# Second pass of a split feed-forward layer: 512-token chunks, and seven block products of two ff tiles in place of eight

## The chip, the cores and the metric

The kernel runs on one core of a Trainium2 chip. Its five engines run side by side, each in the order of its own queue: TensorE (PE, matmuls into the PSUM banks; its weight loads are listed apart as PEld), VectorE (DVE), ScalarE (ACT), GpSimd (POOL, which works on SBUF alone here) and SyncE (SP), from which all transfers are issued. The metric is the device time of one execution in microseconds (us), as the median of three runs.

## The reference

Attention over 8 batches, 8 heads, 576 positions and 64 dimensions, with a causal window of 128, gives x, 4608 tokens by 512. Then follows a feed-forward layer with 2048 hidden columns:

```python
x = np.ascontiguousarray(attn_out.transpose(0, 2, 1, 3)).reshape(B * S, H * D)
h = x @ w_in                                  # 4608 x 2048
sp = np.maximum(h, 0.0) + np.log1p(np.exp(-np.abs(h)))
g = h * erf(sp)
return (g @ w_out).astype(np.float32)         # 4608 x 512
```

## The kernel before

The weights come as double-precision words and are rounded on the chip. Every matmul of the feed-forward layer is made of three passes, since an operand is split in a high part and the rest: high by high, high by rest, rest by high. So `whi`/`wli` are the two parts of a tile of w_in, `who`/`wlo` of w_out, `xh`/`xl` of x, and `gh`/`gl` of g.

Hidden columns are worked in 16 tiles of 128 ("ff tiles"), in two passes over the tokens, since the weights of all 16 don't fit beside the attention. The **first pass** takes tiles 0 to 5 and is woven into the attention; its partial results go to DRAM (`pd`). When the attention's buffers are closed, the weights of tiles 6 to 15 are prepared in their place, and the **second pass** takes these ten and adds the stored part. The changed piece is the second pass.

A chunk is 384 tokens (`CH`), so there are 12 chunks. For each chunk and ff tile there is one unit: twelve matmuls of 384 columns into one PSUM bank (`h`, line 782: four blocks of 128 rows of x, three passes each), a copy of the bank to `hs` by ACT or DVE (lines 766, 768), softplus and erf on ACT with a table load ahead of each (lines 811, 813; four units share a pair of table loads), a product on DVE (line 824), the rounding to `gh` (766, 768) and the rest `gl` (829), and nine matmuls of 512 columns (`o`, line 844: three tiles of 128 tokens, three passes each) that are summed over the ff tiles in three banks. At the end of a chunk each bank is added to the stored part (line 864) and leaves.

The order of all this is not written out. Every operation is entered with the engines that may do it, an assumed duration, the buffers that it reads and writes, and a due time; a planner (`Plan.run`) then lists the operations engine by engine, the earliest due first among those whose inputs and buffers are free. `at` is the due time. `hs`, `s`, `gh` and `gl` live in one pool of 17 buffers of 768 columns (tag `m`, `MB`), where `keep` says how many must stay free when one is taken. x is read into one buffer (`xr`) and split into `xh` and `xl`, three buffers each. `Weights.prepare` does the work for one tile of weights: one pass on ACT, four on DVE, one sum on POOL, then high part and rest (lines 670 to 692).

In PSUM the second pass uses two banks for h and three for o. The three banks of the attention stand empty by then.

Of the kernel before, what the change touches and what calls it, by code (L numbers as in the profile page):

```python
# [39 lines left out]
MB, KH, KS = 17, 4, 2  # L40
PB, XB, OB, TB, TBB = 8, 3, 3, 2, 2
# [268 lines left out]
def pool_tt(n):  # L310
    return 0.15 + n * 0.0025
# [334 lines left out]
class Weights:  # L646
# [9 lines left out]
    def prepare(self, which, f, at, after=()):  # L656
# [3 lines left out]
        q = Buf(self.stage, [P, DM], I32, "wq", 1, f"wq{nm}")  # L660
# [27 lines left out]
        op({"Act": act(DM), "DVE": dve(DM, True)}, lambda e: (  # L688
            nc.scalar.copy if e == "Act" else nc.vector.tensor_copy)(hi.all, flt(t)),
            r=[t, *after], w=[hi], at=at)  # L690
        op({"Pool": pool_tt(DM), **({"DVE": dve(DM)} if WLO else {})}, lambda e: (
            nc.gpsimd if e == "Pool" else nc.vector).tensor_tensor(lo.all, flt(t), hi.all, SUB),  # L692
            r=[t, hi, *after], w=[lo], at=at)
        self.t[which, f] = (hi, lo)


class Moe:
# [4 lines left out]
    def __init__(self, tc, plan, ctx, x_dram, part_dram, out):  # L702
# [11 lines left out]
        self.rounds = []  # L714
        for n, size, tail in zip((NF1, NF - NF1), UPR, ((), TAIL)):
            n = n * nch - sum(tail)
            self.rounds += [size] * (n // size) + [n % size] * (n % size > 0) + [*tail]

    def one_pass(self, weights, first, time):

        fs = weights.ffs
        for c in range(self.nch):
            at = time(self.U)
            x = self.load_x(c, first, at)
            po = [Buf(self.ps_o, [P, DM], F32, f"o{t}", 1, f"o{t}_{self.U}") for t in range(NTT)]
            for f in fs:
                u = self.unit(c, f, weights, x, po, f == fs[0], f == fs[-1], first, time(self.U))
                self.round.append(u)
                self.U += 1
                if len(self.round) == self.rounds[0]:  # L730
                    self.rounds.pop(0)
                    self.flush()

    def direct(self, c):

# [232 lines left out]
```

## Time and profile before

| | us |
|---|---|
| median of 3 runs | 1116.16 |
| lowest, highest | 1114.83, 1118.36 |
| the profiled execution: its time | 1118.25 |
| the profiled execution: its span in the trace | 1116.3 |
| last product of the attention starts (line 596, output `px`) | 521.8 |
| PE busy in the 112 us from 784 on | 112.00 |
| DVE, ACT busy in the same stretch | 40.43, 58.48 |

The span is the time from the first to the last event of the trace, and the execution's own time is a little longer. A matmul's duration in a row holds its way through the array, so rows of successive matmuls overlap: what a matmul costs in a dense stream is the distance from its start to the next one's start. "Busy" of PE is thus no proof of a dense stream, and the distances are. The rows that carry the argument stand in the prediction.

### The profile page before, as it was taken

How to read it: one execution, taken by the hardware profiler on the slowest of the kernel's cores; microseconds unless marked ns; L12 is line 12 of the kernel's file. 1: busy time of each engine (PE TensorE's matmuls, PEld its weight loads, DVE VectorE, ACT ScalarE, POOL GpSimd, SP SyncE). 2: the span in 40 equal slices, each digit the busy share in tenths (PEclk: the TensorE clock that was granted, in tenths of full speed). 3: DMA queues.
4: the chain of work that ended last, by engine and by line, in shares of the span. 5: the costliest groups of instructions: out<-in, count | busy, mean ns of one | idle time of the engine just before them, and what ended most of it. 6: DMA issues, size and time to landing. Idle time of an engine off the chain costs nothing.

```text
span 1116.3 us, 17069 instructions
## 1 busy us (share of the span) xinstructions
PE 1073.7 (96%) x6000; PEld 976.5 (87%) x6000; DVE 684.9 (61%) x1602; ACT 721.9 (65%) x1436; POOL 385.7 (35%) x464
## 2 busy tenths in 40 slices
PE   9776979999999999999999999999999999999998
PEld 8666968988899999999899998899999999999996
DVE  5878898887888888775867675333433433433332
ACT  6567667878788787776677675355455455455462
POOL 5776887646666566653333231000000000000000
PEclk9797999999999999999999999999999999999999
DMA  6444555444545455422343422202202202202102
GB/s 184 139 132 122 140 152 153 146 132 115 163 118 135 121 143 149 118 89 78 114 132 114 141 69 74 86 13 73 85 19 67 85 19 67 85 13 73 57 19 67
DMA packets 89732, 111.59 MB, mean 100 GB/s; under 512 B 45744, under 2 KB 59696, under 8 KB 89648
## 3 DMA queue, kind: packets, MB, share of 16 engines
q1 hardware_dynamic: 89648, 110.52, 33.5%
q8 instruction: 47, 0.77, 0.3%
q14 instruction: 37, 0.30, 0.1%
HBM read 82.18 MB, written 28.31 MB: 99 GB/s over the span
## 4 chain that ended last, share of the span: by engine, by line
PE 82%; DVE 9%; POOL 3%; DMA 2%; issue 2%; ACT 2%; POOLq 0%; SPq 0%; DVEq 0%; ACTq 0%
PE o L844 32%; PE h L782 31%; PE px L596 7%; PE s L511 5%; PE t L578 5%; POOL p L560 2%; DMA xr<-xd 2%; DVE p L522 1%; PE warm_ps L383 1%; DVE xl L759 1%; POOL wto L686 1%; DVE hs L824 1%; DVE gl L829 1%; PE s L497 1%; ACT p L532 1%
## 5 line engine op out<-in xcount | busy, mean ns | idle before, releaser
L782 PE MATMUL h<-xh,whi 128*128 128x384 f32 x768 | 262.5, 342 | 0.0
L782 PE MATMUL h<-xl,whi 128*128 128x384 f32 x768 | 259.2, 338 | 1.6 <-DVE xl L759 1.6
L782 PE MATMUL h<-xh,wli 128*128 128x384 f32 x768 | 259.7, 338 | 0.0
L560 POOL TENSOR_SCALAR p<-p,st 128x256 f32<-128x256 f32 (+2 forms) x320 | 194.0, 623 | 128.1 <-DVE st L550 108.1
L844 PE MATMUL o<-who,gh 128*128 128x512 f32 x576 | 228.8, 397 | 0.6 <-DVE ot L768 0.6
L844 PE MATMUL o<-who,gl 128*128 128x512 f32 x576 | 227.6, 395 | 1.2 <-DVE gl L829 1.2
L844 PE MATMUL o<-wlo,gh 128*128 128x512 f32 x576 | 227.3, 395 | 1.2 <-POOL wlo L692 0.7
L766 ACT COPY hs<-h 128x384 f32<-128x384 f32 x137 | 65.3, 477 | 215.1 <-PE h L782 214.6
L532 ACT ACTIVATE p<-p,st 128x256 f32<-128x256 f32 (+2 forms) x320 | 149.0, 468 | 24.5 <-DVE st L522 23.6
L782 PEld LDWEIGHTS h<-xl,whi 128*128 128x128 f32 x768 | 145.2, 189 | 8.7 <-DVE xl L759 2.1
L782 PEld LDWEIGHTS h<-xh,whi 128*128 128x128 f32 x768 | 145.3, 189 | 6.9 <-ACT hs L766 0.2
L782 PEld LDWEIGHTS h<-xh,wli 128*128 128x128 f32 x768 | 144.8, 189 | 0.2 <-POOL wli L692 0.2
L844 PEld LDWEIGHTS o<-who,gl 128*128 128x128 f32 x576 | 108.1, 188 | 25.4 <-DVE gl L829 2.1
L522 DVE CUSTOM_DVE_ANT_0 p<-s,bias_sb 128x256 f32<-128x256 f32 (+2 forms) x320 | 109.4, 378 | 33.4 <-PE s L511 21.6
L768 DVE COPY hs<-h 128x384 f32<-128x384 f32 x55 | 30.4, 554 | 160.8 <-PE h L782 160.8
L844 PEld LDWEIGHTS o<-wlo,gh 128*128 128x128 f32 x576 | 108.5, 188 | 17.9 <-POOL wlo L692 2.2
L844 PEld LDWEIGHTS o<-who,gh 128*128 128x128 f32 x576 | 108.6, 188 | 16.6 <-DVE ot L768 1.5
L824 DVE TENSOR_TENSOR hs<-s,hs 128x768 f32<-128x768 f32 x96 | 95.2, 1016 | 23.4 <-ACT s L813 23.4
L829 DVE TENSOR_TENSOR gl<-hs,gh 128x768 fp32r<-128x768 f32 x96 | 94.6, 989 | 15.5 <-ACT gh L766 14.7
L578 PE MATMUL t<-ident,p 128*128 128x128 f32 x544 | 85.7, 284 | 17.6 <-POOL p L560 11.8
L578 PEld LDWEIGHTS t<-ident,p 128*128 128x128 f32 x544 | 65.6, 147 | 30.4 <-POOL p L560 14.6
L466 POOL TENSOR_TENSOR a_None<-qr_None,a_None 64x576 fp32r<-64x576 f32 x48 | 76.4, 1592 | 25.7 <-DVE a_None L474 20.7
(80 smaller groups left out, 1653.1 us busy)
## 6 DMA issues: line engine op xcount, KB each, us to landing
xr<-xd SPq DMA_DIRECT2D x22, 768.0 KB, 4.3
kr_None<-k_t SPq DMA_DIRECT2D x48, 288.0 KB, 4.2
pd<-ot SPq DMA_DIRECT2D x36, 256.0 KB, 3.7
ot<-pd SPq DMA_DIRECT2D x36, 256.0 KB, 3.0
wri<-w_in SPq DMA_DIRECT2D x16, 512.0 KB, 3.8
wro<-w_out SPq DMA_DIRECT2D x16, 512.0 KB, 3.7
out_dram<-ot SPq DMA_DIRECT2D x32, 256.0 KB, 2.1
qr_None<-q_t SPq DMA_DIRECT2D x24, 288.0 KB, 3.1
```

The costliest lines, as they stand in the source:

```text
L466: op({"Pool": pool_tt(nq)}, lambda e, j=j, own=own, other=other: nc.gpsimd.tensor_tensor(a[j][other, :nq], q[own, :nq], a[j][own, :nq], SU ...
L511: nc.tensor.matmul(ps[:m, j, :n], lhsT=a[j][:, q0 : q0 + m], rhs=rhs[:, k0 : k0 + n], start=(o == 0), stop=(o == 1),)
L522: nc.vector.tensor_tensor_reduce(out=pt[:m, c0:c1, j, :], in0=blocks(src[j][0][:m, src[j][1], :n]), in1=blocks(self.bias[:m, c0 * 64 : c1 ...
L532: nc.scalar.activation(dst, dst, AF.Exp, bias=low[:m, j : j + 1], scale=-1.0, accum_out=total[:m, j : j + 1],)
L560: nc.gpsimd.tensor_scalar(dst, dst, totals[t][:m, j : j + 1], 1.0, op0=ALU.mult, op1=ALU.mult)
L578: nc.tensor.matmul(ps[:, col : col + P], lhsT=p[t][:, kb].rearrange("p j d -> p (j d)"), rhs=self.ident[:, :], is_transpose=True, start=no ...
L596: self.nc.tensor.matmul(dst[:, q0 - base : q1 - base], lhsT=v[:, blk], rhs=sb[sbi][:, off : off + q1 - q0], start=(blk == order[0][0]), st ...
L766: self.nc.scalar.copy(out, src)
L782: nc.tensor.matmul(ps[:, :CH], lhsT=ww[:, cs], rhs=xx[:, k], start=(k2 + k + n == 0), stop=(k2 + k + n == 4),)
L824: V if e == "DVE" else G).tensor_tensor(hs[:, :n], s[:, :n], hs[:, :n], ALU.mult),
L829: V if e == "DVE" else G).tensor_tensor(gl[:, :n], hs[:, :n], gh[:, :n], SUB),
L844: nc.tensor.matmul(po.all, lhsT=g[:, j, cs], rhs=w.all, start=(u["start"] and n == 0), stop=(u["end"] and n == 2),)
```

## The change

The second pass takes 512 tokens at a time (nine chunks), and two ff tiles together (five pairs for each chunk, 45 pairs in all). For a pair, h is a product of a 2 by 2 block matrix (two ff tiles by two halves of x's 512 rows) and another (the two halves of x's rows by two halves of the tokens). Each of the eight block products was six matmuls; now there are seven block products, of sums and differences of blocks (Strassen's scheme in Winograd's form). Their results are put together with adds.

- **Weights.** `pair` makes, from two rounded tiles, three of the four blocks as they are and four sums (S1 to S4), each with a high part and a rest. They stand where all weights of the second pass stood. The second pass's w_out tiles now go into the buffers of the first pass's weights, which are free when the first pass has used them for the last time.
- **x.** `second_x` loads 512 tokens (from two of the 384-token pieces), makes four differences T1 to T4 and splits seven blocks (`xb` 0 to 6: B11, T1, B21, T2, B22, T3, T4). Four of them lie in a pool of six, three in the pool `m`, as do the differences themselves.
- **h.** A product is six matmuls of 256 columns into half a PSUM bank (`b`); two products share a bank. Four banks take turns: the two of before and two of the attention's. Two products are copied, five are added on DVE straight from PSUM, and two adds have both inputs in SBUF (DVE or POOL).
- **After h.** Softplus, erf, product and split are done on 1024 columns for each pair, with two table loads each. The o products are the same three passes of 512 columns, on four token tiles (the fourth bank is the attention's third).
- **Buffers.** `m` has 12 buffers of 1024 columns in place of 17 of 768, for the first pass too. The due times of the second pass are set anew (`TN`, `XL2`, `XS2`).

```diff
-FIT = 8
-UPR = (4, 4)
-TAIL = (2, 2)
+UPR = 4
+CH2, HALF = 512, 256
-MB, KH, KS = 17, 4, 2
-PB, XB, OB, TB, TBB = 8, 3, 3, 2, 2
+MB, KH, KS, KX = 12, 4, 2, 4
+PB, XB, OB, TB, TBB = 8, 6, 3, 2, 2
...
-        q = Buf(self.stage, [P, DM], I32, "wq", 1, f"wq{nm}")
+        q = Buf(self.stage, [P, DM], I32, "wq", 2, f"wq{nm}")
...
+    def pair(self, f, values, at, after):
...
+        (ta, flt), (tb, _) = (self.rounded(0, f + i, at) for i in range(2))
+        sums = Buf(values, [P, 4, HALF], F32, "m", MB, f"ws{f}", keep=KX)
+        pool, tag = self.place(0, f)
+        hi = Buf(pool, [P, 7, HALF], F32R, "h" + tag, 1, f"wh{f}")
+        lo = Buf(pool, [P, 7, HALF], F32R, "l" + tag, 1, f"wl{f}")
...
+        for k, x, y, sub, r in (
+            (0, lambda: flt(tb)[:, one], lambda: flt(tb)[:, two], False, [tb]),
+            (1, lambda: S(0), lambda: flt(ta)[:, one], True, [ta, parts[0]]),
+            (2, lambda: flt(ta)[:, one], lambda: flt(tb)[:, one], True, [ta, tb]),
+            (3, lambda: flt(ta)[:, two], lambda: S(1), True, [ta, parts[1]]),
+        ):
...
+    def second_x(self, d, at):
...
+        raw = Buf(self.xp, [P, NK, CH2], F32, "xr", 1, f"xr{d}_2")
...
+            pool, tag, bufs, keep = (self.xp, "xs", XB, None) if k < 4 else (self.hp, "m", MB, KX)
+            both = Buf(pool, [P, 2, 2, HALF], F32R, tag, bufs, f"xb{d}_{k}", keep=keep)
...
+        split("B11", 0)
+        sub("T1", 0, "B12", "B11")
+        split("T1", 1)
+        split("B21", 2)
+        sub("T2", 1, "B22", "T1")
+        split("T2", 3)
+        split("B22", 4)
+        sub("T3", 2, "B22", "B12")
+        split("T3", 5)
+        sub("T4", 3, "B21", "T2")
+        split("T4", 6)
...
+    def second_pair(self, Q, d, f, weights, x, po, spare, start, end, at):
...
+        hs = Buf(self.hp, [P, 2, CH2], F32, "m", MB, f"hs_q{Q}", keep=KH)
...
+            i, half = divmod(self.P, 2)
+            self.P += 1
+            if not half:
+                pool, tag, n = ((self.ps_h, "h", 2), (self.ps_h, "h", 2), (spare, "t", 1), (spare, "x", 1))[i % 4]
+                self.bank = Buf(pool, [P, 512], F32, tag, n, f"b{i}")
+            to = Part(self.bank, slice(None), slice(half * HALF, (half + 1) * HALF))
...
+            def mm(e):
+                for kk in range(2):
+                    cs = slice(kk * P, (kk + 1) * P)
+                    for n, (ww, xx) in enumerate(((hi, xh), (hi, xl), (lo, xh))):
+                        nc.tensor.matmul(
+                            to.all, lhsT=ww[:, k, cs], rhs=xx[:, kk],
+                            start=(kk + n == 0), stop=(kk + n == 3),
+                        )
...
+        copy(h11, product("A11", "B11", x["T4"]))
+        add(h12, product("S2", "T2"), h11)
+        add(h21, product("S3", "T3"), h12)
+        copy(h22, product("S1", "T1"))
+        add(h11, product("A12", "B21"), h11)
+        add(h12, h12, h22)
+        add(h22, h21, h22)
+        add(h21, product("A22", "T4"), h21)
+        add(h12, product("S4", "B22"), h12)
+        g = self.values([(f"_q{Q}", 2, CH2, [*H.values()], hs, at + MC)], False)[0]
+        for j in range(2):
+            last = end and j == 1
+            for t in range(NT2):
+                self.products(weights.t[1, f + j], j, t, g, po[t], start and j == 0, last, at + MP)
...
     place = lambda k, f: (
-        (pool2, f"{k}_{f}") if f < NF1 + FIT else (w1p, f"{k}_{f - NF1 - FIT}")
+        (pool2, f"2_{f}") if k == 0 else (w1p, f"{(f - NF1) // NF1}_{(f - NF1) % NF1}")
     )
```

How the change moves instructions is seen at three places. A row gives the line, the operation, output and inputs with the number of each buffer, the size, and a count of equal rows. First PE in the middle of the second pass of before: the o group of one unit ends, and the h group of the next begins.

```order
L844 MATMUL o_142_9655<-who_7413,gh_9606 128x512
L844 MATMUL o_142_9655<-wlo_7420,gh_9606 128x512
L844 MATMUL o_142_9655<-who_7413,gl_9612 128x512
L782 MATMUL h_9726<-xh_0_9424,whi_6551 128x384
L782 MATMUL h_9726<-xl_0_9433,whi_6551 128x384
L782 MATMUL h_9726<-xh_0_9424,wli_6572 128x384
```

PE now, where the second pass goes from its third chunk to its fourth: the end of the last product of the old chunk (`xb_4_8301`), then the first three products of the new chunk's first pair (T2, T1 and B21).

```order
L994 MATMUL b_8774<-xb_4_8301,wh_7012 128x256 x2
L994 MATMUL b_8774<-xb_4_8301,wl_7024 128x256
L994 MATMUL b_8783<-xb_3_8722,wh_6563 128x256 x2
L994 MATMUL b_8783<-xb_3_8722,wl_6566 128x256
L994 MATMUL b_8783<-xb_3_8722,wh_6563 128x256 x2
L994 MATMUL b_8783<-xb_3_8722,wl_6566 128x256
L994 MATMUL b_8793<-xb_1_8398,wh_6563 128x256 x2
L994 MATMUL b_8793<-xb_1_8398,wl_6566 128x256
L994 MATMUL b_8793<-xb_1_8398,wh_6563 128x256 x2
L994 MATMUL b_8793<-xb_1_8398,wl_6566 128x256
L994 MATMUL b_8793<-xb_2_8715,wh_6563 128x256 x2
```

A matmul is narrower, and its weights change as often as before. Two products stand behind each other in one bank (`b_8793`). Behind these rows follow, in this order: the rest of that product, two groups of three o matmuls, the product with `xb_5`, two groups, the one with the new `xb_4`, ten groups, and the products with `xb_0` and `xb_6`, which end the first pair of the new chunk.

DVE of before, where the second half of a chunk's x is split (`xl_1_9383`) between products and rests of g.

```order
L824 TENSOR_TENSOR hs_9284<-s_9314,hs_9284 128x768
L759 TENSOR_TENSOR xl_1_9383<-xr_0_9086,xh_1_9375 128x768
L829 TENSOR_TENSOR gl_9393<-hs_9227,gh_9378 128x768
L829 TENSOR_TENSOR gl_9405<-hs_9284,gh_9385 128x768
L768 CAST xh_0_9424<-xr_0_9391 128x768
L759 TENSOR_TENSOR xl_0_9433<-xr_0_9391,xh_0_9424 128x768
```

DVE now, at the same change from the third chunk to the fourth as on PE. `hs_q_8696` and `hs_q_8751` are the last two pairs of the old chunk.

```order
L1010 TENSOR_TENSOR hs_q_8751<-b_8774,hs_q_8751 128x256
L808 CAST xb_5_8811<-xt_1_8790 128x512
L940 TENSOR_TENSOR xb_5_8811<-xt_1_8790,xb_5_8811 128x512
L872 TENSOR_TENSOR hs_q_8696<-s_q_8764,hs_q_8696 128x1024
L1010 TENSOR_TENSOR hs_q_8751<-b_8755,hs_q_8751 128x256
L808 CAST gh_q_8837<-hs_q_8696 128x1024
L879 TENSOR_TENSOR gl_q_8849<-hs_q_8696,gh_q_8837 128x1024
L808 CAST xb_0_8857<-xr_2_8808 128x512
L940 TENSOR_TENSOR xb_0_8857<-xr_2_8808,xb_0_8857 128x512
L872 TENSOR_TENSOR hs_q_8751<-s_q_8839,hs_q_8751 128x1024
L808 CAST xb_6_8879<-xt_1_8790 128x512
L940 TENSOR_TENSOR xb_6_8879<-xt_1_8790,xb_6_8879 128x512
```

The adds from PSUM are new on DVE, and the x of a chunk is made in seven pieces, the last of them (`xb_6`) behind two products that wait for ACT.

More of the change, by code (lines that the diff above doesn't have):

```diff
@@ L687, in prepare @@
            r=[q, t], w=[t], at=at)
[L688 to L693, printed above, removed]
-        self.t[which, f] = (hi, lo)
+        return t, flt
@@ new lines, in split @@
+    def split(self, n, src, hi, lo, r, at, after=()):
+        nc, op = self.nc, self.plan.op
+        op({"Act": act(n), "DVE": dve(n, True)}, lambda e: (
+            nc.scalar.copy if e == "Act" else nc.vector.tensor_copy)(hi.all, src()),
+            r=[*r, *after], w=[hi], at=at)
+        op({"Pool": pool_tt(n), **({"DVE": dve(n)} if WLO else {})}, lambda e: (
+            nc.gpsimd if e == "Pool" else nc.vector).tensor_tensor(lo.all, src(), hi.all, SUB),
+            r=[*r, hi, *after], w=[lo], at=at)
@@ L713, in __init__, with first_pass @@
         self.round = []
[L714 to L719, printed above, removed]
+    def first_pass(self, weights, time):
         fs = weights.ffs
@@ L802, in flush @@
             us = units[k : k + 2]
-            n = len(us)
-            hs, U, at = us[0]["hs"], us[0]["U"], us[0]["at"] + MC
-            s = Buf(self.hp, [P, 2, CH], F32, "m", MB, f"s{U}", keep=KS)
-            pairs.append((us, n, n * CH, hs, s, at))
-        first = units[0]["first"]
+            pairs.append((us[0]["U"], len(us), CH, [us[0]["hs"]], us[0]["hs"], us[0]["at"] + MC))
+        for (U, n, ch, _, hs, at), g in zip(pairs, self.values(pairs, True)):
+            for j, u in enumerate(units[U - units[0]["U"] :][:n]):
+                for t in range(NTT):
+                    self.products(u["w"], j, t, g, u["po"][t], u["start"], u["end"], u["at"] + MP)
+                    if u["end"]:
+                        self.store_part(u["U"], self.part[u["c"]][t], u["po"][t], u["at"] + MP)
@@ new lines, in values, with products @@
+        return out
+    def products(self, w, j, t, g, po, start, end, at):
+        wh, wl = w
+        gh, gl = g
+        def mm(e):
+            cs = slice(t * P, (t + 1) * P)
+            for n, (g, w) in enumerate(((gh, wh), (gh, wl), (gl, wh))):
+                self.nc.tensor.matmul(
+                    po.all, lhsT=g[:, j, cs], rhs=w.all, start=(start and n == 0), stop=(end and n == 2),
+                )
+        self.plan.op({"PE": 3 * f32r_us(DM) + 0.015}, mm, r=[gh, gl, wh, wl], w=[po], at=at)
@@ new lines, in second_pass @@
+    def second_pass(self, weights, spare, time):
+        fs = weights.ffs
+        Q = self.P = 0
+        for d in range(len(self.x_dram) * CH // CH2):
+            x = self.second_x(d, time(Q))
+            po = [
+                Buf(self.ps_o, [P, DM], F32, f"o{t}", 1, f"o{t}_d{d}") if t < NTT
+                else Buf(spare, [P, DM], F32, "s", 1, f"o{t}_d{d}") for t in range(NT2)
+            ]
+            for f in fs[::2]:
+                self.second_pair(Q, d, f, weights, x, po, spare, f == fs[0], f == fs[-2], time(Q))
+                Q += 1
@@ new lines, in store_part, with store, rows @@
+    def store_part(self, U, part, po, at):
+        nc, op = self.nc, self.plan.op
+        ot = Buf(self.op_, [P, DM], F32, "o", OB, f"ot_{part.name}_{U}")
+        op({"DVE": dve(DM), "Act": act(DM, src=0.13)},
+           lambda e: self.copy(e, ot.all, po.all), r=[po], w=[ot], at=at)
+        op(emit=lambda e: nc.sync.dma_start(part.ap, ot.all), r=[ot], w=[part], at=at, **dma(P * DM * 4))
+    def store(self, nm, c, t, po, at):
+        nc, op = self.nc, self.plan.op
+        ot = Buf(self.op_, [P, DM], F32, "o", OB, f"ot{nm}")
+        part = self.part[c][t]
+        op(emit=lambda e: nc.sync.dma_start(ot.all, part.ap), r=[part], w=[ot], at=at - 10,
+           **dma(P * DM * 4))
+        op({"DVE": dve(DM)}, lambda e: nc.vector.tensor_tensor(
+            ot.all, po.all, ot.all, ALU.add), r=[po, ot], w=[ot], at=at)
+        def rows(e):
+            for o, r0, n in rows_of(c, t):
+                nc.sync.dma_start(self.out[r0 : r0 + n, :], ot[o : o + n])
+        op(emit=rows, r=[ot], at=at, **dma(P * DM * 4, len(rows_of(c, t))))
```

218 lines of the change are left out of this document (135 added, 83 removed).

## The prediction, made before the changed kernel was run

> **What bounds the kernel now.** I read the page first: busy shares, and the chain of work that ended last.
>
> ```profile
> PE 1073.7 (96%) x6000; PEld 976.5 (87%) x6000; DVE 684.9 (61%) x1602; ACT 721.9 (65%) x1436; POOL 385.7 (35%) x464
> ...
> PE 82%; DVE 9%; POOL 3%; DMA 2%; issue 2%; ACT 2%; POOLq 0%; SPq 0%; DVEq 0%; ACTq 0%
> PE o L844 32%; PE h L782 31%; PE px L596 7%; PE s L511 5%; PE t L578 5%; POOL p L560 2%; DMA xr<-xd 2%; DVE p L522 1%; PE warm_ps L383 1%; DVE xl L759 1%; POOL wto L686 1%; DVE hs L824 1%; DVE gl L829 1%; PE s L497 1%; ACT p L532 1%
> ```
>
> The feed-forward matmuls carry 63% of the chain. The change is in the second pass, so I ask that part, and the hand-over to it, for the busy time of each stretch.
>
> ```profile
> core 0: us, PE busy (x) PEld busy (x) DVE busy (x) ACT busy (x) POOL busy (x), PEclk, DMA share, GB/s
> 504.00:560.00 56.00, 54.55 (x290) 48.51 (x290) 38.80 (x66) 34.50 (x61) 19.23 (x19) 1.00 0.28 92
> 560.00:616.00 56.00, 56.00 (x284) 50.89 (x283) 41.17 (x57) 42.79 (x55) 18.84 (x14) 1.00 0.38 122
> 616.00:672.00 56.00, 56.00 (x294) 52.07 (x293) 37.12 (x60) 39.00 (x54) 18.61 (x14) 1.00 0.35 113
> ...
> 896.00:1008.00 112.00, 112.00 (x562) 101.39 (x562) 41.32 (x51) 58.03 (x74) 0.00 (x0) 1.00 0.16 52
> ```
>
> PE never rests from 560 on, at a full granted clock (1.00), while DVE is busy 41.32 of 112 us and ACT 58.03. The chain in the second pass alternates between two lines.
>
> ```profile
> 923.54 2.10 PE h L782 x12
> 925.65 2.08 PE o L844 x9
> 927.73 2.10 PE h L782 x12
> 929.84 2.08 PE o L844 x9
> 931.92 2.10 PE h L782 x12
> ```
>
> A unit takes 927.73 - 923.54 = 4.19 us, 2.10 for h and 2.08 for o, with no third thing between. So the second pass is bound by the rate of matmuls: its 120 units are 120 x 4.19 = 503 us. A saving in h's matmuls counts in full, as long as nothing else gets late.
>
> **The matmuls.** Removed: 120 x 12 of 384 columns, 120 x 2.10 = **252.0 us**. Added: 45 pairs x 7 products x 6 = 1890 of 256 columns. The pass has none of these, but the attention's scores are of that shape and type, each with its own weight load.
>
> ```profile
> 301.19 0.27 PE L511 MATMUL s<-kl_None,a_None 128*128 128x128 f32 x1
> 301.30 0.27 PE L511 MATMUL s<-kh_None,a_None 128*128 128x128 f32 x1
> 301.41 0.28 PE L511 MATMUL s<-kl_None,a_None 128*128 128x128 f32 x1
> ...
> 303.62 0.28 PE L511 MATMUL s<-kl_None,a_None 128*128 128x256 f32 x1
> 303.74 0.28 PE L511 MATMUL s<-kh_None,a_None 128*128 128x256 f32 x1
> 303.86 0.28 PE L511 MATMUL s<-kl_None,a_None 128*128 128x256 f32 x1
> 303.98 0.34 PE L782 MATMUL h<-xh,whi 128*128 128x384 f32 x1
> ```
>
> Starts lie 0.12 us apart at 256 columns and 0.11 at 128. Half the columns save a tenth: near 0.11 something other than columns sets the pace. I take 0.12, a product 6 x 0.12 = 0.72 us, 315 products **226.8 us**. The bounds are 0.11 (207.9 us, if the 128-column spacing could be had here) and 0.125 (236.3, two hundredths of reading error over three matmuls). The columns fall by an eighth, the time by a tenth. The o products are 1080 of 512 columns as before, at 2.08 / 9. So PE saves 252.0 - 226.8 = **25.2 us**.
>
> What the floor of 0.11 is, the weight loads show.
>
> ```profile
> 301.24 0.19 PEld L511 LDWEIGHTS s<-kh_None,a_None 128*128 128x128 f32 x1
> 301.35 0.19 PEld L511 LDWEIGHTS s<-kl_None,a_None 128*128 128x128 f32 x1
> ```
>
> Loads follow each other at 0.11 us too, though a row says 0.19. The Trainium skill, "TensorE: Matmul & The Clock Gate", section "LDWEIGHTS (loading the stationary operand)", gives columns / 1.2 ns, an estimate of 107 ns for 128 columns; the rows agree. That speaks against narrow blocks, since a 256-column product has almost no time left over its load. The Trainium skill, same page, section "Back-to-back issue gap", gives columns / 2.4 + 2.5 ns, an estimate of 109 ns at 256; by it the products would take 206 us and the saving be 46 us. The measured 0.12 is longer, and decides.
>
> **The work beside it.** Durations by engine in the second pass, all shapes apart:
>
> ```profile
> L829 DVE TENSOR_TENSOR gl<-hs,gh 128x768 fp32r<-128x768 f32 x52 | 49.2, 954 | 14.5 <-ACT gh L766 13.8
> L824 DVE TENSOR_TENSOR hs<-s,hs 128x768 f32<-128x768 f32 x52 | 48.3, 964 | 15.5 <-ACT s L813 15.5
> L811 ACT ACTIVATE s<-hs 128x768 f32<-128x768 f32 x54 | 42.7, 837 | 0.3
> L766 ACT COPY hs<-h 128x384 f32<-128x384 f32 x76 | 36.4, 479 | 186.5 <-PE h L782 186.5
> L811 ACT ACT_TABLE_LOAD x27 | 34.6, 1283 | 0.5
> L864 DVE TENSOR_TENSOR ot<-o,ot 128x512 f32<-128x512 f32 x30 | 20.7, 691 | 50.2 <-PE o L844 50.1
> L768 DVE CAST xh<-xr 128x768 fp32r<-128x768 f32 x13 | 7.3, 560 | 26.2 <-PE h L782 14.8 <-DMA xr<-xd 11.4
> ```
>
> ```profile
> 304.64 0.42 DVE L522 CUSTOM_DVE_ANT_0 p<-s,bias_sb 128x256 f32<-128x256 f32 x1
> ```
>
> The last row is a 256-column operation from PSUM with a second input, which is what an add of a product is: 0.42 us. By columns, a product or rest on 1024 is 4/3 x 0.96 = 1.27, softplus or erf 4/3 x 0.837 = 1.12, a 512-column rest of an x block 2/3 x 0.95 = 0.64, its rounding on DVE 2/3 x 0.56 = 0.37.
>
> A pair takes PE 7 x 0.72 + 8 x 0.693 = 10.6 us (0.693 is an o group of three). DVE's part of a pair: five adds from PSUM 2.1, product and rest of g 2.54, one SBUF add 0.42, and, as its order gives them out (28 of 45 roundings of g at 0.75, 27 copies at 0.42, 36 stores at 0.69, 62 x operations at 0.64 and 21 at 0.37), 2.3 more: 7.4 us, or 70%. ACT: two table loads 2.57, two functions 2.23 and about 1.8 of copies and roundings: 6.6, or 62%. Both fit under PE, so all the new elementwise work is costed at nothing; uncovered, DVE's 2.1 of adds alone would be 45 x 2.1 = 95 us. POOL's few operations here are under 2 us a pair.
>
> Fitting on average isn't enough, so I went along the queues where cover is thinnest, at the change from the third to the fourth chunk shown above. Let 0 be the end of the old chunk's last product. ACT finishes the softplus and erf of the old chunk's fourth pair at about 3.3 (4.8 from the copy of its fifth pair's T1 product at -1.5). After a 0.36 copy come those of the fifth pair, to about 8.6. DVE in between does the product, an add, the rounding and the rest for the fourth pair, and splits `xb_0`, until about 9.1. Then follow product (1.27), rounding (0.37) and rest (0.64) to `xb_6` at **11.4**. PE reaches the product with `xb_6` after six products and 14 o groups, 6 x 0.72 + 14 x 0.693 = **14.0**. 2.6 us are over. A new chunk's raw x (a 4 us transfer) is asked for one whole chunk early, as soon as the old differences are made, so it isn't late either.
>
> ```profile
> xr<-xd SPq DMA_DIRECT2D x22, 768.0 KB, 4.3
> ```
>
> The other chunk changes have the same make-up. Between a pair's last product and its first o matmul, PE's order has at least 16 us of other work everywhere, against a chain of 0.42 + 2.57 + 2.23 + 1.27 + 0.75 + 1.27 = 8.5. So I put no stall there.
>
> **The hand-over** is less safe. DVE is busy 38.80 + 41.17 + 37.12 = 117 of the 168 us from 504 to 672. There the change adds about 12 us of weight sums and wider roundings, 11 for two chunks of x and some 17 of adds: 157, or 93%. The w_out tiles must also wait for the first pass's buffers, but are first used 28 us of PE work after the first product. I charge **3 us**, between nothing and the 11 us that are left there. The first pass keeps its matmuls; its order gives the same 660 h matmuls before the attention's end as before, and 435 o matmuls for 438, so the 12 buffers cost nothing that I can see. The last pair's cover at the end is 16 us, and the last stores are as before.
>
> **Sum.** -25.2 + 3 = -22.2 us. For the profiled execution, 1118.25 (its span of 1116.3 and 2 us around it) becomes 1096. It lies 2.1 above the median of the three, so the median is predicted at **1094**.
>
> **Rivals.**
>
> 1. *The narrow matmul is quicker than I read*, at 0.11: 207.9 us in place of 226.8, so about 1075. For it: columns alone would allow it. Against: every dense pair of 256-column rows above has 0.12. By the gap formula of the Trainium skill, cited above, it would be about 1073.
> 2. *The hand-over leaks* 5 to 17 us more because DVE at 93% is late with x or weights: 1099 to 1111. For it: the stretch is the fullest of the kernel. Against: PE has o work in store there.
> 3. *No gain.* At each of eight chunk changes PE waits 22.2 / 8 = 2.8 us for an x block, just more than the 2.6 us that were over: about 1116. It needs every change to be 5.4 us worse than worked out. If it is worse by more, the result is slower.
> 4. *Slower: a bank that is written holds its reader, or the other way round.* Before, no bank of the second pass is written by PE while DVE reads it. Now the second product goes into one half of a bank while the first is read from the other. If PE had to wait for each read, 157 banks x 0.42 = 66 us would come on: 1160. It decides from 22.2 / 157 = 0.14 us a bank. No row here shows such an overlap, so the cost lies between 0 and 66; I take 0, since PE's order has no wait there and only a hidden hold could cost. The Trainium skill, "PSUM — Partial Sum Buffer", section "PSUM bank collisions raise a hardware error", says that the chip does not arbitrate or stall in this case; by it this rival costs no time, and no run here shows it yet.
>
> **Chances.** Forecast, 1084 to 1104: 0.70. Rival 1: 0.04. Rival 2 beyond 1104: 0.10. Rival 3 within 0.3%: 0.05; past it: 0.04. Rival 4: 0.07. A measurement of this kernel tells some 0.3%, 3.3 us, from no change. Faster: 0.70 + 0.04 + 0.10 = 0.84; same 0.05; slower 0.11. The range 1083 to 1111 holds the forecast with the bounds of its products (0.115 to 0.125) and rival 2.
>
> **What would show it.** Right: 256-column `b` rows 0.12 apart, seven products in 5.0 us, pairs 10.6 us apart, PE dense between 620 and the end, DVE near 70%. Wrong: gaps on PE ahead of products with waits released by DVE or ACT (rivals 2, 3 by their place), or a product over 0.72 us without any release (rival 4, or a slower matmul than read).

## The result and the profile after

| | us |
|---|---|
| before, median of 4 runs | 1117.26 |
| after, median of 4 runs | 1146.38 |
| ratio, 95% interval | 1.0264 (1.0232 to 1.0297) |
| span of the profiled execution, before and after | 1116.3 and 1145.0 |

The change makes the kernel 2.6% slower; 1094 was predicted. First the page of after: busy shares, then the chain that ended last.

```profile
PE 1061.6 (93%) x6450; PEld 956.4 (84%) x6450; DVE 864.5 (76%) x1902; ACT 737.8 (64%) x1431; POOL 500.0 (44%) x551
PE 64%; DVE 21%; DMA 5%; issue 4%; ACT 3%; POOL 2%; SPq 0%; DVEq 0%; POOLq 0%; ACTq 0%
```

PE had 82% of the chain before and has 64% now; DVE went from 9% to 21%. POOL's busy time grew from 385.7 to 500.0 us. The same stretches as before, by windows, tell where:

```profile
504.00:560.00 56.00, 50.87 (x277) 46.46 (x276) 41.38 (x71) 35.47 (x69) 27.92 (x24) 0.94 0.23 75
560.00:616.00 56.00, 46.28 (x215) 38.80 (x214) 52.95 (x64) 30.39 (x44) 36.17 (x21) 0.97 0.34 115
616.00:672.00 56.00, 41.63 (x230) 35.88 (x229) 52.40 (x68) 34.56 (x46) 35.96 (x24) 0.88 0.37 122
784.00:896.00 112.00, 110.55 (x688) 99.39 (x687) 76.91 (x124) 63.01 (x70) 17.23 (x16) 1.00 0.19 60
```

From 560 to 672 PE is busy 88 of 112 us, where it was busy all the time before, and DVE 105 of 112. POOL is busy 72 us there, twice the 37 of before. In the middle of the second pass PE is nearly dense and DVE at 76.91 / 112 = 69%. The hand-over and what follows it, of before and then of after:

```profile
525.00:690.00 165.00, 163.48 (x827) 147.92 (x826) 121.43 (x175) 117.00 (x150) 53.89 (x38) 1.00 0.33 108
690.00:1090.00 400.00, 400.00 (x2002) 361.66 (x2001) 142.38 (x176) 208.12 (x263) 0.00 (x0) 1.00 0.17 55
```

```profile
525.00:690.00 165.00, 134.67 (x685) 116.61 (x683) 145.86 (x184) 96.45 (x129) 98.71 (x60) 0.93 0.30 98
690.00:1090.00 400.00, 393.74 (x2451) 353.95 (x2452) 279.97 (x452) 223.00 (x247) 61.00 (x58) 1.00 0.18 56
```

A ledger of the 28.7 us of span, used for every run below. "Last px" is the start of the last rows of the attention's last product in PE's timeline. "Gaps" are the sum of what the starts of successive matmuls lie further apart than 0.12, 0.175 and 0.231 us (256, 384 and 512 columns); where they lie a little closer, that is taken off, and "none" is a sum of nothing or less. "Tail" is the time from the start of the last matmul to the end. (Expectations below put last px of after at 524.7; the row starts at 524.54.)

| | before | after | difference |
|---|---|---|---|
| products (120 x 2.10 against 315 x 0.72) | 252.0 | 226.8 | -25.2 |
| last px | 520.77 | 524.54 | +3.8 |
| gaps, last px to 690 | 3.1 | 43.2 | +40.1 |
| gaps after 690 | 0.2 | 7.5 | +7.3 |
| tail | 5.2 | 8.4 | +3.2 |

The sum is +29.2, where the span grew by 28.7. The 40 us decide. No single waiter has them: these are PE's waits from 520 to 690 in after.

```profile
PE o L892 <- DVE gl L879: 6.8, 5, 2.9
PE h L822 <- ACT hs L806: 5.6, 3, 2.7
PE b L994 <- DVE hs_q L1010: 4.5, 2, 3.8
PE b L994 <- DVE xb L940: 3.8, 1, 3.8
PE o L892 <- DVE gh L808: 2.9, 1, 2.9
```

PE waits mostly for whatever DVE has queued. All its waits in this stretch come to 29 us. Of the rest of the 43, about 8 us are matmuls that run slower. The granted clock is 1.00 throughout this stretch in before; in after it is 0.50 in five pieces between 546.3 and 648.7 us, 24 us together. The longest, and what follows it:

```profile
638.50:648.70 10.20, 5.37 (x19) 4.46 (x20) 10.20 (x12) 3.09 (x5) 7.20 (x6) 0.50 0.23 94
648.70:660.00 11.30, 11.30 (x82) 10.63 (x81) 10.97 (x21) 8.18 (x10) 5.25 (x4) 1.00 0.32 95
```

In the first of them matmuls of 256 columns start 0.21 us apart (646.64 and 646.85) in place of 0.12. So a wait can cost more than its own length. That the clock falls because PE waits is argued from these two kernels; no run tests it alone.

So the question is why DVE is late. Its groups in this stretch, all shapes apart: two of before, then the same two of after.

```profile
L829 DVE TENSOR_TENSOR gl<-hs,gh 128x768 fp32r<-128x768 f32 x21 | 21.5, 1025 | 1.0 <-ACT gh L766 0.9
L673 DVE TENSOR_SCALAR wti<-wqi 128x512 int32<-128x512 int32 x8 | 5.4, 676 | 3.0 <-ACT wqi L670 3.0
```

```profile
L879 DVE TENSOR_TENSOR gl<-hs,gh 128x768 fp32r<-128x768 f32 x10 | 16.0, 1596 | 0.0
L676 DVE TENSOR_SCALAR wti<-wqi 128x512 int32<-128x512 int32 x8 | 10.9, 1380 | 0.0
L1010 DVE TENSOR_TENSOR hs_q<-b,hs_q 128x256 f32<-128x256 f32 x24 | 9.7, 417 | 3.8 <-ACT hs_q L806 1.5 <-PE b L994 1.3 <-POOL hs_q L1010 0.7
```

The same rest takes 1.60 us in the mean instead of 1.03, the same shift 1.38 instead of 0.68. The add from PSUM, with one operand in SBUF, does not stretch (0.417). The timelines of DVE and of POOL in after show the pattern:

```profile
565.13 2.62 DVE L676 TENSOR_SCALAR wti<-wqi 128x512 int32<-128x512 int32 x1
567.66 0.41 DVE L680 TENSOR_SCALAR wqi<-wti 128x512 int32<-128x512 int32 x1
```

```profile
564.68 2.78 POOL L697 TENSOR_TENSOR wl<-ws,wh 128x1024 fp32r<-128x1024 f32 x1 [0.96 <-DVE wh L693]
```

Two DVE operations of one kind and size: the one that starts under a POOL operation takes 2.62 us and ends 0.3 us behind it, and the next takes 0.41. The trace of before already has such pairs, here two shifts of DVE and the POOL operation under which the second one starts:

```profile
587.71 0.43 DVE L673 TENSOR_SCALAR wti<-wqi 128x512 int32<-128x512 int32 x1 [0.83 <-ACT wqi L670]
595.82 1.52 DVE L673 TENSOR_SCALAR wto<-wqo 128x512 int32<-128x512 int32 x1
```

```profile
595.18 1.87 POOL L692 TENSOR_TENSOR wli<-wti,whi 128x512 fp32r<-128x512 f32 x1 [1.53 <-PE h L782]
```

That is **Theory 1**: while POOL works on SBUF it holds DVE's operations whose operands lie in SBUF. The rivals are that the added work is too much wherever it is done (amount), that it stands in the wrong order, or that the twelve `m` buffers are too few.

### The profile page after: what moved, and what is told of

Its sections match the earlier page's. It is cut to its first block, busy times and chain, and to the rows that moved or that the text cites. A ratio compares the mean times of both kernels' runs of the same rounds, so it can differ in the third digit from the quotient of the medians.

```text
span 1145.0 us, 18583 instructions
## 1 busy us (share of the span) xinstructions
PE 1061.6 (93%) x6450; PEld 956.4 (84%) x6450; DVE 864.5 (76%) x1902; ACT 737.8 (64%) x1431; POOL 500.0 (44%) x551
## 4 chain that ended last, share of the span: by engine, by line
PE 64%; DVE 21%; DMA 5%; issue 4%; ACT 3%; POOL 2%; SPq 0%; DVEq 0%; POOLq 0%; ACTq 0%
PE o_d L892 19%; PE b L994 17%; PE h L822 8%; PE o L892 6%; PE px L598 5%; PE s L513 4%; PE t L580 4%; DMA xr<-xd 2%; DVE xb L940 1%; DVE p L524 1%; DVE gl L879 1%; POOL p L562 1%; DVE hs L872 1%; DVE xb L808 1%; DVE hs_q L1010 1%
## 5 line engine op out<-in xcount | busy, mean ns | idle before, releaser
L994 PE MATMUL b<-xb,wh 128*128 128x256 f32 x1260 | 236.1, 286 | 16.6 <-DVE xb L940 10.8
L994 PEld LDWEIGHTS b<-xb,wh 128*128 128x128 f32 x1260 | 203.6, 193 | 29.3 <-DVE xb L940 13.8
L994 PE MATMUL b<-xb,wl 128*128 128x256 f32 x630 | 179.4, 285 | 0.0
L534 ACT ACTIVATE p<-p,st 128x256 f32<-128x256 f32 (+2 forms) x320 | 149.4, 469 | 25.8 <-DVE st L524 25.2
L892 PE MATMUL o_d<-who,gh_q 128*128 128x512 f32 x360 | 141.3, 393 | 1.3 <-ACT ot_None L806 0.8
L892 PE MATMUL o_d<-who,gl_q 128*128 128x512 f32 x360 | 140.2, 390 | 1.5 <-DVE gl_q L879 1.5
L892 PE MATMUL o_d<-wlo,gh_q 128*128 128x512 f32 x360 | 141.1, 392 | 0.0
L822 PE MATMUL h<-xh,whi 128*128 128x384 f32 x288 | 101.7, 353 | 5.7 <-ACT hs L806 5.6
L822 PE MATMUL h<-xl,whi 128*128 128x384 f32 x288 | 99.1, 344 | 2.4 <-DVE xl L799 2.4
L822 PE MATMUL h<-xh,wli 128*128 128x384 f32 x288 | 99.4, 345 | 0.4 <-POOL wli L697 0.4
L892 PE MATMUL o<-wlo,gh 128*128 128x512 f32 x216 | 87.4, 405 | 2.4 <-POOL wlo L697 2.4
```

What stands on the lines that cost most here:

```text
L534: nc.scalar.activation(dst, dst, AF.Exp, bias=low[:m, j : j + 1], scale=-1.0, accum_out=total[:m, j : j + 1],)
L822: nc.tensor.matmul(ps[:, :CH], lhsT=ww[:, cs], rhs=xx[:, k, :CH], start=(k2 + k + n == 0), stop=(k2 + k + n == 4),)
L892: self.nc.tensor.matmul(po.all, lhsT=g[:, j, cs], rhs=w.all, start=(start and n == 0), stop=(end and n == 2),)
L994: nc.tensor.matmul(to.all, lhsT=ww[:, k, cs], rhs=xx[:, kk], start=(kk + n == 0), stop=(kk + n == 3),)
```

## The experiments

All are compared with the kernel before, run on the same chip (medians 1116.0 to 1117.1). Times and spans are in us.

| run | median | ratio, 95% | last px | gaps to 690 | gaps after | DVE, POOL busy 525-690 |
|---|---|---|---|---|---|---|
| before | 1117.3 | 1 | 520.8 | 3.1 | 0.2 | 121, 54 |
| after | 1146.4 | 1.023-1.030 | 524.5 | 43.2 | 7.5 | 146, 99 |
| e1_no_pool | 1116.8 | 0.997-1.001 | 523.1 | 15.3 | 8.1 | 125, 24 |
| e2_on_act | 1127.9 | 1.007-1.013 | 520.8 | 28.3 | 6.9 | 121, 22 |
| e3_pool_twice | 1193.2 | 1.065-1.071 | 522.5 | 77.8 | 21.3 | 151, 133 |
| e11_before_twice | 1148.1 | 1.025-1.030 | 520.0 | 26.6 | 6.2 | 132, 103 |
| e10_no_sums | 1127.0 | 1.006-1.012 | 521.6 | 26.5 | 6.4 | 145, 76 |
| e4_before_12 | 1133.7 | 1.012-1.017 | 529.5 | 10.7 | 0.3 | 119, 55 |
| e5_dve_only | 1134.7 | 1.013-1.019 | 521.9 | 41.8 | none | 142, 84 |
| e9_due_later | 1145.2 | 1.022-1.028 | 523.0 | 43.7 | 6.8 | 150, 102 |
| e6_dve_weights | 1137.2 | 1.016-1.019 | 527.4 | 38.0 | none | 131, 22 |
| e8_last_ot | 1133.5 | 1.013-1.018 | 525.9 | 38.4 | none | 131, 22 |
| e12_no_late_pool | 1122.9 | 1.003-1.008 | 530.1 | 28.9 | none | 134, 4 |
| e13_spread | 1125.1 | 1.006-1.010 | 526.0 | 22.3 | 5.9 | 138, 0 |
| e14_after_13 | 1148.7 | 1.025-1.031 | 526.4 | 43.6 | 8.7 | 143, 96 |
| e15_dve_13 | 1122.0 | 1.003-1.007 | 517.9 | 34.3 | none | 138, 2 |
| e16_dve_13_spread | 1105.6 | 0.987-0.993 | 518.8 | 21.0 | none | 141, 0 |

**POOL's part.** e1 leaves POOL's work for the second pass's weights out, e2 puts ACT copies in its place, e3 issues it twice.

```diff
 # e1: rounding's sum and the rests left out, the high part multiplied for the rest
-op({"Pool": pool_tt(DM)}, lambda e: nc.gpsimd.tensor_tensor(flt(t), flt(t), flt(q), ALU.add),
+op({"Pool": pool_tt(DM)}, lambda e: None if second else nc.gpsimd.tensor_tensor(...
 # e2
+    nc.scalar.copy(flt(t), flt(q)) if second else nc.gpsimd.tensor_tensor(...
 # e3
+    nc.gpsimd.tensor_tensor(lo.all, src(), hi.all, SUB) for _ in range(2 if self.ffs[0] >= NF1 else 1)
```

> Left out: everything that POOL does for the second pass's weights (the sum that ends the rounding, and the rests; the matmuls take the high part in place of the rest; the few weight sums that POOL made are copies on ACT). The order of DVE is unchanged. Theory 1, POOL's operations hold DVE's over the hand-over (DVE busy 158 us from 525 to 690, of which some 109 at undisturbed durations): DVE's rows fall back to their short durations, PE's gaps from 525 to 690 (43 us) shrink below 10, time 1100 to 1116. Theory 2, DVE has too many operations there whatever POOL does: the gaps stay above 30, time 1135 or more. Theory 3, the weights come late through their chain of steps and few staging buffers: between the two, 1115 to 1135, with DVE idle in the hand-over.

> The same POOL operations of the second pass's weights stand at the same places in the program, but as copies on ACT (the sum and the difference are left out), so the chain of steps and the waits for it stay. Theory 1 (POOL holds DVE): DVE's rows short again, gaps below 15, time 1104 to 1122, a little behind the run without them since ACT gets some 29 us more. Theory 2 (too many DVE operations): above 1135. Theory 3 (chain of steps): above 1130, as the chain is as long as before.

> Every POOL operation of the second pass's weights is issued twice (the second sum writes a buffer that nobody reads any more; the rest is written twice alike): some 50 us more on POOL over the hand-over, nothing more on DVE. Theory 1: 50 us x (49 us of stretching / 100 us of POOL work in the hand-over now) = 25 us more, 1160 to 1185, DVE's rows longer still. Theory 2: DVE's work is the same, 1143 to 1152. Theory 3: POOL's part of the chain doubles, 1150 to 1165 with DVE idle waiting for POOL.

Without it the loss of 29 us is gone, with copies on ACT in its place 18 of the 29 go, and doubled it costs 47 more. All three move the way that Theory 1 says, but none hits its numbers: e1 has 15.3 us of gaps for less than 10, e2 28.3 for less than 15, and e3 costs 47 us where 25 were worked out. In e1 the shifts and rests on DVE are back at their undisturbed times:

```profile
L885 DVE TENSOR_TENSOR gl<-hs,gh 128x768 fp32r<-128x768 f32 x10 | 9.5, 952 | 0.0
L679 DVE TENSOR_SCALAR wti<-wqi 128x512 int32<-128x512 int32 x8 | 3.2, 422 | 0.4 <-ACT wqi L676 0.4
```

That speaks for Theory 1, but e1 also leaves work out, so it doesn't exclude amount. e2 leaves no step out: its copies on ACT stand where POOL's operations stood, and DVE's shifts and rests are short there too (0.42 and 0.95 in the mean). What stretched them is thus POOL's work and not the number of steps. 9.5 us of e2's waits are for ACT, which has the copies on top. And e1 only draws level with before: its gaps to 690 stay at 15.3, where the prediction had put 3, and 8.1 stay behind 690.

The kernel before shows whether it was near the same edge. e11 is before with the rounding's sum and the rests on POOL issued twice.

> The kernel before, with POOL's operations for the second pass's weights (the rounding's last sum and the rests) issued twice: 40 more operations of 128x512, of 1.1 us each when undisturbed, on an engine that is idle for two thirds of this stretch. If POOL and VectorE ran beside each other, this would cost nothing to 5 us: time 1116 to 1121. If each holds the other (Theory 1), the kernel before stands as near to the edge as the changed one: VectorE's operations stretch, PE's gaps from the last px to 690 us rise from 3 to 15 to 45, time 1130 to 1160.

It loses 31 us, within Theory 1's range. Two rests of g from DVE's timeline there, and what POOL did:

```profile
565.04 0.94 DVE L833 TENSOR_TENSOR gl<-hs,gh 128x768 fp32r<-128x768 f32 x1
585.33 1.88 DVE L833 TENSOR_TENSOR gl<-hs,gh 128x768 fp32r<-128x768 f32 x1 [0.31 <-ACT gh L770]
```

```profile
566.67 1.29 POOL L687 TENSOR_TENSOR wti<-wti,wqi 128x512 f32<-128x512 f32 x1 [4.51 <-DVE wqi L678]
...
585.11 1.29 POOL L687 TENSOR_TENSOR wti<-wti,wqi 128x512 f32<-128x512 f32 x1 [4.51 <-DVE wqi L678]
586.48 1.89 POOL L689 TENSOR_TENSOR wqi<-wti,wqi 128x512 f32<-128x512 f32 x1
```

The first ran while POOL was idle (its idle time ends at 566.67), the second under two POOL operations: 0.94 and 1.88 us. Nothing was added to DVE, and POOL at 103 of 165 us is far from full, yet the end moves by 31 us. Not all of that is the hold on DVE: 7.1 of the 19 us that PE waits from 520 to 690 are for `wlo`, the rests that POOL itself now writes twice. Either way the idle two thirds of POOL were not free for use in the kernel before.

e10 leaves out only what the change adds to the weights: the four sums of a pair (high parts are then copies of other blocks) and their rests.

```diff
-            (3, 4, lambda: sums.all, parts),
+            (3, 2, lambda: flt(ta).rearrange("p (k n) -> p k n", k=2), [ta]),
+            (5, 2, lambda: flt(tb).rearrange("p (k n) -> p k n", k=2), [tb]),
-            self.split(n * HALF, src, h, l, r, at, after)
+            self.split(n * HALF, src, h, None if k0 >= 3 else l, r, at, after)
```

> The changed kernel without the four sums of a pair's weight blocks and without the rests of these four: their high parts are copies of other blocks, and where their rests would be multiplied the high parts are. Each pair of ff tiles loses 1024 columns of sums (POOL and VectorE) and 1024 of rests (POOL); what POOL and VectorE do for the second pass's weights is then at most what they do in the kernel before, while seven blocks, twelve m buffers and the second pass are as in the changed kernel. Theory 4 (the amount that the change adds to VectorE and POOL): PE's gaps in the hand-over fall from 43 to 10 to 20 us, as without any of POOL's work (15.3), time 1112 to 1125. Rival (what is new in the weights is small beside the buffers and the x differences): gaps 30 to 43, time 1133 to 1146.

19 of the 29 us go, between the two forecasts in gaps (26.5) and in time. Two thirds of the loss come with the sums and their rests, that is with the amount of work that the change adds for POOL and DVE; one third is there without them.

**Buffers.** e4 is the kernel before with `MB` 12 for 17.

> The kernel before with 12 instead of 17 of the buffers tagged m, and nothing else. In the changed kernel the attention's last px product came 3.9 us later than before (524.7 against 520.8 by the merged rows), although the change says nothing of the first pass but this number. Theory A (the buffers): the first pass's values wait for a free buffer, so the engines' order differs and the attention ends later: px end 523 to 526, and the time goes up by about as much, 1119 to 1122. Theory B (something else delays the attention: the second pass's weight work, which POOL begins before the attention ends): px end 520.5 to 521.5, time 1116 to 1118.

It loses 16.7 us, more than either theory said: the attention ends 8.7 us later and 7.6 us of gaps appear in the hand-over. Waits for the weights `who` and `wlo` are 5.3 us there, and there are none in before. So the number of buffers is worth a lot, to the kernel before. Whether it is to the changed one, e14 asks below.

**Order.** e9 moves the weights' due times in the planner, with the same operations.

```diff
-W2A, W2B = 60, 2.0
+W2A, W2B = -20, 3.0
```

> The changed kernel with the second pass's weights due later and spread wider in the planner (W2A, W2B = -20, 3 instead of 60, 2): the same operations, with the first pass's own activations ahead of the weights in VectorE's and ScalarE's order for longer. Theory 3 (order: the weights stand ahead of what PE waits for in queues that run in order): PE's gaps from the last px to 690 us fall from 43 to 25 or less, time 1120 to 1130. Theory 4 (amount: VectorE and POOL together have more to do in this stretch than it holds, in whatever order): gaps stay at 35 to 50, only elsewhere, time 1138 to 1155.

Gaps stay at 43.7 and the time at 1145. With POOL's work as it is, this other order changes nothing.

**Steady state.** e5 takes POOL's choice away from the second pass's x differences and rests and from the adds within `hs`.

```diff
-op({"DVE": dve(2 * HALF), "Pool": pool_tt(2 * HALF)}, ...
+op({"DVE": dve(2 * HALF)}, ...
-            if src.whole is hs:
-                engines["Pool"] = pool_tt(HALF)
```

> The second pass's differences of x, rests of x and adds within hs may go to DVE alone, not POOL; results unchanged. From 690 on PE has 10 us of gaps, ahead of products that wait for x blocks split on DVE. Theory 1 (POOL's 1.5 us operations hold DVE at the chunk changes): gaps from 690 on below 4 us, time 1136 to 1143. Theory 2 (volume): DVE gets some 35 us more there, gaps of 15 us or more, 1150 or more.

DVE is given more to do, and the gaps after 690 vanish. PE's one wait there in after, and the one that is left in e5:

```profile
PE b L994 <- DVE xb L940: 7.0, 8, 1.4
```

```profile
PE b L994 <- DVE hs_q L1008: 0.4, 2, 0.2
```

The eight waits lie at four of the eight chunk changes, two at each (from 742, 850, 957 and 1065 us on). Ahead of them POOL makes three differences of x in a row, and DVE's roundings, 0.42 us in e5, take more than three times as long, as here on DVE and on POOL in after:

```profile
738.54 1.46 DVE L808 CAST xb<-xt 128x512 fp32r<-128x512 f32 x1
739.91 1.52 DVE L808 CAST xb<-xr 128x512 fp32r<-128x512 f32 x1
```

```profile
738.42 1.29 POOL L925 TENSOR_TENSOR xt<-xr,xt 128x512 f32<-128x512 f32 x1 [5.50 <-PE b L994]
739.67 1.48 POOL L925 TENSOR_TENSOR xt<-xr 128x512 f32<-128x512 f32 x1
```

So they are Theory 1 too, in the second pass. The hand-over keeps its 41.8.

**POOL's work moved to DVE.** e6 is e5 with the second pass's weights on DVE as well, e8 adds another buffer for the last stored part, and e12 takes POOL out of the last three chunks of the first pass (values, and rests of x).

```diff
 # e6
+op({"DVE": dve(DM)} if f >= NF1 else {"Pool": pool_tt(DM)}, ...
+op({"DVE": dve(n)} if self.ffs[0] >= NF1 else {"Pool": pool_tt(n)}, ...
 # e8
+if (c, t) == (self.nch - 1, NTT - 1):
+    ot = Part(Buf(self.xp, [P, NK, CH2], F32, "xr", 1, f"ot{nm}"), slice(None), 0)
 # e12
+late = not first or U >= LATE * NF1
+op({"DVE": dve(n2)} if late else {"DVE": dve(n2), "Pool": pool_tt(n2)}, ...
```

> As e5_dve_only, and beside it the second pass's weights make no use of POOL: the rounding's last sum, the weight sums and the rests are VectorE's. Same result, and VectorE is given more operations than in any run so far: its undisturbed durations between the last px and 690 us come to some 109 us in the changed kernel, and POOL's work there, worth some 45 us more on VectorE, makes about 153 of 165 us. Theory 1 (POOL holds VectorE while it runs, each stretches the other): VectorE's operations return to their undisturbed durations (the 512-word shifts to 0.41 to 0.45 us), the gaps of PE in that stretch fall from 41.8 us (e5) to 8 to 20, time 1100 to 1115, faster than the kernel before. Theory 2 (VectorE has simply too much to do in the hand-over, whoever else works): more work on VectorE makes it worse, gaps 40 to 60, time 1130 to 1150.

> As e6_dve_weights, and the very last token tile's stored part is loaded into the buffer that held raw x (free by then), instead of waiting for one of the three output buffers. In the changed kernel that load was issued at 1138.41 us, after the first store of the last chunk, and the last add waited 4.32 us for it; from the last product to the end of the span it took 8.4 us, before 5.2. Theory: the wait for the buffer is the whole of the difference: 5 to 5.5 us from the last product to the end, and the time 2.5 to 3.5 us under e6_dve_weights. Rival (the end is set by the four adds and the stores' own landing): 7.5 to 8.5 us, the time within 1 us of e6_dve_weights.

> As e8_last_ot, and the last three of the first pass's twelve chunks use VectorE alone for x's rests and for the activations' product and rest: after the attention POOL has nothing left to do. In e6_dve_weights one such POOL operation (768 columns, 1.97 us elsewhere) took 10.8 us at 581 us beside a busy VectorE, and PE waited 10.2 us for it. Theory 1 (what is left of the 38 us is this hold): the gaps of PE from the last px to 690 us fall to 20 to 28, time 1117 to 1125. Theory 4 (amount: VectorE has no room for it either): gaps 33 to 42, time 1130 to 1138.

e6 missed: DVE's shifts are nearly back (0.42 to 0.65 in the mean), but the gaps fall only to 38, and the time lies in the range of Theory 2. One of its POOL operations shows that the hold goes both ways; the last two rows are DVE's:

```profile
548.04 2.01 POOL L800 TENSOR_TENSOR xl<-xr,xh 128x768 fp32r<-128x768 f32 x1
567.19 3.59 POOL L880 TENSOR_TENSOR gl<-hs,gh 128x768 fp32r<-128x768 f32 x1 [17.14 <-ACT gh L807]
581.12 10.81 POOL L880 TENSOR_TENSOR gl<-hs,gh 128x768 fp32r<-128x768 f32 x1 [10.34 <-DVE gh L809]
...
589.31 0.96 DVE L880 TENSOR_TENSOR gl<-hs,gh 128x768 fp32r<-128x768 f32 x1
590.58 2.17 DVE L800 TENSOR_TENSOR xl<-xr,xh 128x768 fp32r<-128x768 f32 x1 [0.31 <-ACT xh L807]
```

768 columns take POOL 2.0 us or 10.8, by what DVE does meanwhile, and PE waited 10.2 us for the last. From 581.12 on DVE starts fourteen operations without a pause. Its first pause is the 0.31 us ahead of 590.58; then its own operation is the long one, and POOL's ends at 591.93. e12 takes such operations away, and 10.6 us of time with them. The hold is still not all: with nearly no POOL in the stretch 28.9 of the 43.2 us of gaps remain. What of these is the amount of work on DVE, now 134 of 165 us, and what the order in which PE waits for it, stays open. e8's buffer shortens the tail from 8.2 to 5.0, as expected.

**What was left.** e12 still stood 6 us behind before. e13 spreads the weights (`W2A, W2B = 0, 7`); e14 is the changed kernel, and e15 is e12, with `MB` 13 and `XB` 5; e16 is e15 with `W2A, W2B = 0, 9`.

> As e12_no_late_pool, with the second pass's weights due at W2A, W2B = 0, 7 in the planner instead of 60, 2: the pairs' weights then lie some 14 planner microseconds apart, so that those of the last pairs are made while the first pairs are multiplied, and VectorE's work spreads to about 690 us. Theory 4 (amount in this stretch): gaps fall by 5 to 15 us against e12_no_late_pool, time 1115 to 1128. Rival (order is worth nothing, as e9_due_later showed for the changed kernel): within 4 us of e12_no_late_pool.

> The changed kernel with 13 instead of 12 buffers tagged m, the 4 KB taken from x's buffers (XB 5 instead of 6), and nothing else. Theory B (buffers: the change's loss is in good part the five m buffers that it gave up, as e4_before_12 lost 16 us by it): the attention ends at 521 to 523, PE's gaps to 690 us fall by 8 or more, time 1130 to 1140. Theory 4 with Theory 1 (POOL and VectorE have no room, whatever the buffers): within 6 us of the changed kernel, 1140 to 1152.

> e12_no_late_pool with 13 m buffers and XB 5. There POOL no longer holds VectorE, and the first pass came out 5 us later than in the changed kernel (last px 530.1 against 524.7) with 28.9 us of gaps behind it. Theory B (buffers set both): last px 520 to 523, gaps 18 to 26, time 1106 to 1115, faster than before. Rival (the later px is VectorE's, which took POOL's work for the chunks that overlap the attention): px stays at 527 to 531, time 1119 to 1126.

> e15_dve_13 with the weights due at W2A, W2B = 0, 9 instead of 60, 2, so that a pair's weights are made some 18 planner microseconds after the pair before. In e13_spread the same move (0, 7) took 6.6 us of gaps out of the hand-over and put 8 back behind 690 us. If order is worth something once POOL is out of the way and buffers are there: gaps to 690 us fall to 10 to 18, time 1095 to 1108. If not: within 4 us of e15_dve_13.

One more `m` buffer (for one less of x) gives the changed kernel nothing (e14), and by itself hardly anything to e12: px comes 12 us earlier, but the gaps behind it grow from 28.9 to 34.3, and the median of ten runs is 1 us lower. (Its profiled execution is 6 us shorter, but that compares its fastest run with the slowest of e12.) Spread alone (e13) moves gaps to behind 690. Both together, with POOL out of the way, give 1105.6: faster than before by 1.0% (0.7 to 1.3). e16 also differs from e13 in 9 for 7, so how much of its 19 us is the buffer and how much that number isn't told apart. Its windows:

```profile
525.00:690.00 165.00, 152.06 (x828) 135.16 (x827) 141.07 (x257) 119.17 (x160) 0.00 (x0) 0.95 0.31 99
690.00:1090.00 400.00, 400.00 (x2497) 361.78 (x2496) 282.73 (x512) 232.31 (x257) 0.00 (x0) 1.00 0.18 59
```

DVE is busy 141 us here, with all that POOL had. In after, DVE and POOL were busy 146 and 99 us, and PE 134.67 for 152.06. So the 99 us of POOL took nothing off DVE's busy time.

## Why the prediction was wrong

1. *The bound and the dense products: right.* Rows of 256 columns lie 0.12 us apart, from 841.04 to 841.40 three of them:

```profile
841.04 0.40 PE L994 MATMUL b<-xb,wh 128*128 128x256 f32 x2
841.28 0.28 PE L994 MATMUL b<-xb,wl 128*128 128x256 f32 x1
841.40 0.40 PE L994 MATMUL b<-xb,wh 128*128 128x256 f32 x2
```

So a product takes 0.72 us and the 25.2 us were saved. Rival 1 (0.11) falls. Rival 4 never came to a test. The prediction took it that one half of a bank is written while the other is read. With the program's buffer numbers put to the rows, none of the 315 readings of a bank runs while its other half is written: 311 start when both products have ended, and four end 13 us or more ahead of the second. The 66 us are not there (7.5 us of gaps in all behind 690, 7.0 of waits for `xb`), but no run here shows what such an overlap would cost.
2. *Elementwise work under the products in the middle of the pass: right in amount* (DVE 69% against 70% predicted, ACT 63.01 / 112 = 56% against 62%).
3. *The chunk changes, "no stall there": wrong by 7 us.* The one worked out by hand, from the third to the fourth, has no wait indeed. What failed is "the other chunk changes have the same make-up": four of the eight wait some 1.5 us each, ahead of the first products of the new chunk (T1, T2, B21) and not of `xb_6`. The durations were undisturbed ones, and POOL's few operations were waved off by their amount ("under 2 us a pair"). e5 shows that they make the wait.
4. *The hand-over, "3 us, between nothing and 11": the step that failed*, by 37 us. Its 157 us for DVE were added up from durations of rows and from the busy time of before, and POOL's new work was left out of the sum, as if it were free. DVE's amount was not exceeded (147 of the 168 us); yet the gaps are 43 us. A good part of what the change adds goes to POOL (54 to 99 us from 525 to 690), and POOL holds DVE. The rows of before show it: its means of 1.03 and 0.68 us were already stretched (0.95 and 0.42 undisturbed). What the runs show in place of the 3 us: without POOL's work for the weights 15.3 us of gaps (e1), with it twice 77.8 (e3), and with all of POOL's work on DVE 28.9 (e12). So the hold is the part that was priced at nothing, and the work itself, wherever it is done, is the other part. What work on POOL costs here is not told by its idle share: e11 adds 40 operations of about 1.5 us, 60 us on an engine that is busy for a third of the stretch, and loses 31. Rival 2 named the place and not the mechanism, and its 17 us were no bound.
5. *"The 12 buffers cost nothing that I can see": wrong.* Counts of matmuls ahead of the attention's end can't show a wait. In the kernel before the five buffers are worth 16.7 us (e4). In the changed kernel 3.8 us of later attention stand beside it, and e14 shows no gain from one more, so how the rest of e4's loss divides here stays open.
6. *"The last stores are as before": wrong by 3.2 us.* A last chunk has four token tiles and three `ot` buffers; the fourth tile's stored part is loaded only when a store has left:

```profile
1136.31 0.70 DVE ot L1046
...
1138.41 2.79 DMA ot<-pd
...
1141.32 0.69 DVE ot L1046
```

e8 shows that the buffer is the whole of it.

The Trainium skill states the rule that I left out, "SBUF — State Buffer", section "Who interferes with whom": VectorE shares a pair of ports with GpSimd; whoever holds it holds it for a whole instruction, and the other waits. By the page this concerns VectorE operations with two inputs in SBUF, and copies, casts and scalar operations in their fast modes, but not one with a single SBUF input outside them. The rows agree with each case: rests with two inputs 0.95 to 2.02 us, shifts 0.41 to 2.62, adds from PSUM 0.42 throughout. The page gives no durations for such operations; these rows do. In one point the measurement goes further than a hold of one instruction: POOL's 10.81 us in e6 cover fourteen instructions of DVE.

## What to carry to other kernels

An engine that the profile shows idle isn't free if it shares a port with a busy one: price new POOL work as if DVE did it, and look in the trace of before for one operation with two durations (the shift at 0.43 and 1.52 us here) ahead of adding any. Where a stretch is as full as this one (DVE 121 of 165 us in before), an amount worked out from mean busy time was no bound; test the stretch itself by doubling the suspect in the kernel before, as e11 did. And a change that is right in its main term can be worth having after its side costs are moved: the seven products were worth 25 us all along, and 10 of them are left once POOL is out, one `m` buffer is back, the last store has a buffer of its own and the weights are spread.

## What was not expected of the hardware

A POOL operation of 768 columns took from 2.0 to 10.8 us beside a busy DVE, so POOL is held as well, and longer than it holds: the longest DVE shift under POOL took 2.6 us. In the hand-over of after the granted clock was 0.50 for 24 us, so PE's waits there were not its only loss. Moving all of POOL's work in the hand-over to DVE did not raise DVE's busy time: 146 us with POOL at 99 in the changed kernel, 134 with POOL at 4 in e12, 141 with POOL at none in e16.
